# One written sequence for every engine in an mLSTM and gated feed-forward kernel

## The chip, the cores and the metric

The kernel runs on one core of one Trainium2 chip. The metric is the device time of one execution in microseconds (us). TensorE (PE) multiplies matrices into PSUM; VectorE (DVE), ScalarE (ACT) and GpSimd (POOL) do elementwise work; SyncE (SP) issues almost all transfers. Each engine runs its own instructions in the order in which the program has them and waits on semaphores for the others. So what this case is about is only the order.

## The reference

Two stages follow each other. The first is a recurrence over 768 time steps for 4 batches of 8 heads with 40 channels; the second is a gated feed-forward layer over the resulting 3072 tokens of 320 channels.

```python
m_new = np.maximum(f_gate[:, :, t] + m, i_gate[:, :, t])
f_stab = np.exp(f_gate[:, :, t] + m - m_new)
i_stab = np.exp(i_gate[:, :, t] - m_new)
C = f_stab[...] * C + i_stab[...] * np.einsum('bhd,bhe->bhde', vt, kt)
n = f_stab[...] * n + i_stab[...] * kt
h_tilde = np.einsum('bhde,bhe->bhd', C, qt)
denom = np.maximum(np.abs(np.einsum('bhd,bhd->bh', n, qt)[:, :, None]), 1.0)
y[:, :, t] = 1.0 / (1.0 + np.exp(-o_gate[:, :, t])) * h_tilde / denom
...
x = attn_out.transpose(0, 2, 1, 3).reshape(B * S, H * D)
gate = 1.0 / (1.0 + np.exp(-(x @ w_gate)))       # 320 x 1536
return (gate * (x @ w_val) @ w_out).astype(np.float32)
```

The weights arrive as 64-bit floats and are decoded on the chip.

## The kernel before

The 768 steps are cut in 6 chunks of 128, and a chunk c with a batch b is a unit; there are 24, numbered u = 4c + b. In a name such as `ks_0_2055` the 0 is the batch and the last number counts buffers. Within a unit the recurrence is worked as matrix products. `st_a` transposes q and k on TensorE (tile `pt`, in three groups of heads). For chunks 0 and 1 the copies are float32 (`qk`, `qbd`). From chunk 2 on they are split in a high and a low part (`kh` on ScalarE, `kl` on VectorE), and SyncE stores both to a scratch tensor `scr` in DRAM and reads them back stacked (`stack`: `ks`, `qs`). `st_b` forms the scores (tile `s`), which VectorE multiplies with the decay matrix `d`; that one is loaded from `mscr`, exponentiated on ScalarE or prepared on GpSimd, and masked on GpSimd. `st_c` adds the old state's part (`in`) and the gather over the unit's own steps (`av`), divides, and makes `x`. `st_d` transposes `x` (tile `xt`) and splits it into `xh` and `xl`, the feed-forward input. `st_e` updates the state `cst` through tile `cs`.

The feed-forward runs in tiles: `ffn_up` makes two products of 16 matmuls in the PSUM tiles `pg0` and `pg1`, ScalarE takes the tanh of pg0 (`sg`), VectorE multiplies with pg1, ScalarE casts (`gh`), VectorE takes the rest (`gl`), and `ffn_down` adds three matmuls per token block to `po`. A full tile has 512 tokens of a chunk; some chunks are cut in half tiles of 256, first for batches 0 and 1, then for 2 and 3. `pg0` and `pg1` have one buffer each. All other PSUM tiles of the recurrence share the two banks of the pool `ps_a`. The weights come in 30 pieces, each decoded by `w_dec`: a pass on ScalarE (`dc`), three on VectorE, a cast on ScalarE (`wh`, the two halves of `w`, `oh`), a subtraction on GpSimd (`wl`, `w`, `ol`).

What sets the order: TensorE's order is written by hand, as a sort of events by the numbers in `PARAM['pe']` (how far the feed-forward has come). The other engines' order is left to a scheduler with priorities (`PARAM['pri']`), except in the opening (the units 0 and 1 and the first three weight pieces), where `PARAM['open']` ranks the steps, and up to the point `PARAM['pin']`. A step such as `w_dec` or `st_c` was called as one, or from one yield to the next, and the scheduler then placed its instructions.

Of the kernel before, what the change touches and what calls it, by code (L numbers as in the profile page):

```python
# [23 lines left out]
    'pos': {  # L24
# [18 lines left out]
    'pin': 0.9829449281013305,  # L43
    'open': {
# [9 lines left out]
        'wvd': 56.338, 'na1': 103.682, 'xt0': 93.253, 'wve': 83.362, 'wrb': 81.994, 'nb1': 87.717, 'wrc': 83.39,  # L54
        'xt1': 75.16, 'wrd': 105.028, 'wre': 108.438, 'kw1': 88.729, 'e2': 123.641,
    },
    'AV': 4,
    'AV0': 4,
    'up': 0.6550267155341185,
    'pri': {  # L60
        'a': 1, 'b': 62, 'c': 0, 'd': 96, 'u': 1,
    },
    'wllate': [0],
    'split': [0, 0, 0, 5, 5, 5],
# [37 lines left out]
    },  # L102
}
GROUPS = ((0, 3), (3, 3), (6, 2))
# [3 lines left out]
def mlstm_then_gated_ffn_kernel(  # L108
# [36 lines left out]
    ps_a = ctx.enter_context(tc.tile_pool(name="ps_a", bufs=2, space=bass.MemoryType.PSUM))  # L145


# [9 lines left out]
    def load_unit(c, b, eng=nc.sync):  # L157
        t0 = c * L

        def src(t):  # L160
            return t[b, :, t0 : t0 + L, :].rearrange("h t d -> t h d")

        u = (c, b)
        qt[u] = big.tile([P, H, D], F32, tag="q", name=f"q_{c}_{b}", bufs=3)
        kt[u] = big.tile([P, H, D], F32, tag="k", name=f"k_{c}_{b}", bufs=3)
        vt[u] = big.tile([P, H, DA], F32, tag="v", name=f"v_{c}_{b}", bufs=3)
        ot[u] = big.tile([P, H, D], F32, tag="o", name=f"o_{c}_{b}", bufs=3)
        eng.dma_start(qt[u], src(q))
        nc.sync.dma_start(kt[u], src(k))
        eng.dma_start(vt[u][:, :, :D], src(v))  # L170
        nc.sync.dma_start(ot[u], src(o_gate))
        nc.gpsimd.memset(vt[u][:, :, D : D + 1], 1.0)
# [205 lines left out]
    def st_a(c, b):  # L378
# [42 lines left out]
        if not unscored:  # L421
            stack()
# [561 lines left out]
```

## Time and profile before

| | us |
|---|---|
| median of 3 runs (568.5 to 571.63) | 569.81 |
| the profiled execution, its own time | 572.92 |
| its span, first to last instruction | 571.2 |
| TensorE busy | 533.2 (93%) |
| VectorE busy | 320.1 (56%) |
| ScalarE busy | 234.1 (41%) |
| GpSimd busy | 159.7 (28%) |

The mean granted TensorE clock is 0.967 of full speed. A line of the profile names a line of the kernel, the engine, the operation and its tiles (out<-in). Behind an instruction, brackets give how long its engine was idle ahead of it and what ended that. The clock column of the views by stretches is the mean granted clock there: 0.50 is half speed.

### The profile page before, as it was taken

Reading aid. Unit: us, or ns where it says so; the run is one execution under the profiler, and the core shown is the slowest. Engines: PE = TensorE matmul, PEld = TensorE weight load, DVE = VectorE, ACT = ScalarE, POOL = GpSimd, SP = SyncE. Lnnn points to the kernel's source line nnn. Section 1 sums busy time; section 2 is a strip of 40 time slices with the busy share of each in tenths; the row PEclk is TensorE's granted clock in tenths of the full one; section 3 lists DMA queues with packets and bytes.
Section 4 is the critical chain, followed back from the end, with each engine's and each line's share of the span. In section 5 each row is a group of like instructions: output and inputs, shape, how many; then the busy total and the mean of one; then the engine's idle time right before and its main releaser. Section 6 shows DMA issues by size and latency. Waiting matters only on the chain.

```text
span 571.2 us, 12202 instructions
## 1 busy us (share of the span) xinstructions
PE 533.2 (93%) x4739; PEld 477.9 (84%) x4739; DVE 320.1 (56%) x739; ACT 234.1 (41%) x581; POOL 159.7 (28%) x231
## 2 busy tenths in 40 slices
PE   8547899899998989999999999999999999999997
PEld 7346797688797989999888888888888888899996
DVE  5798778874852555463655554554643545533322
ACT  5386556644532335343434242343332332232222
POOL 5567435653712006220142220143210210000000
PEclk9678799999997999999999999999999999999999
DMA  9697647222554556745566765666763734010000
GB/s 198 184 240 221 176 137 207 59 77 53 136 174 88 145 124 165 156 143 123 138 148 154 151 177 134 143 147 143 164 174 107 185 79 110 27 36 2 24 2 23
DMA packets 131649, 72.42 MB, mean 127 GB/s; under 512 B 103112, under 2 KB 120776, under 8 KB 131592
## 3 DMA queue, kind: packets, MB, share of 16 engines
q1 hardware_dynamic: 130504, 71.39, 51.2%
q8 instruction: 37, 0.61, 0.5%
q10 hardware_dynamic: 1088, 0.26, 0.2%
q14 instruction: 20, 0.16, 0.1%
HBM read 56.95 MB, written 14.68 MB: 125 GB/s over the span
## 4 chain that ended last, share of the span: by engine, by line
PE 75%; DVE 8%; DMA 5%; POOL 4%; ACT 3%; issue 3%; SPq 1%; POOLq 0%; DVEq 0%; ACTq 0%
PE pg L585 32%; PE pg L590 11%; PE po L610 7%; PE po L614 6%; PE po L612 6%; DMA qs<-scr 4%; PE s L477 2%; PE av L446 2%; PE pt L408 2%; PE in L491 2%; PE xt L533 2%; PE cs L545 1%; DVE dc L297 1%; DVE dc L302 1%; DVE d L469 1%
## 5 line engine op out<-in xcount | busy, mean ns | idle before, releaser
L585 PE MATMUL pg<-xh,wh 128*128 128x256 f32 (+1 forms) x412 | 111.0, 343 | 4.2 <-ACT sg L594 3.0
L585 PE MATMUL pg<-xh,wl 128*128 128x256 f32 (+1 forms) x412 | 108.9, 340 | 0.0
L595 DVE SCALAR_TENSOR_TENSOR sg<-sg,pg 128x256 f32<-128x256 f32 (+1 forms) x103 | 54.1, 525 | 97.0 <-ACT sg L594 96.3
L585 PE MATMUL pg<-xl,wh 128*128 128x256 f32 (+1 forms) x412 | 106.9, 336 | 0.0
L594 ACT ACTIVATE sg<-pg 128x256 f32<-128x256 f32 (+1 forms) x103 | 48.2, 468 | 128.6 <-PE pg L590 128.1
L610 PE MATMUL po<-oh,gh 128*128 128x320 f32 x288 | 91.8, 319 | 0.8 <-ACT gh L598 0.8
L612 PE MATMUL po<-ol,gh 128*128 128x320 f32 x288 | 91.8, 319 | 0.0
L614 PE MATMUL po<-oh,gl 128*128 128x320 f32 x288 | 91.8, 319 | 0.0
L599 DVE TENSOR_TENSOR gl<-sg,gh 128x256 fp32r<-128x256 f32 (+1 forms) x103 | 60.6, 589 | 38.6 <-ACT gh L598 37.8
L585 PEld LDWEIGHTS pg<-xh,wh 128*128 128x128 f32 x412 | 70.9, 194 | 9.2 <-ACT sg L594 4.0
L585 PEld LDWEIGHTS pg<-xh,wl 128*128 128x128 f32 x412 | 70.5, 193 | 6.4
L585 PEld LDWEIGHTS pg<-xl,wh 128*128 128x128 f32 x412 | 70.4, 193 | 6.3
L598 ACT ACTIVATE gh<-sg 128x256 fp32r<-128x256 f32 (+1 forms) x103 | 51.7, 502 | 50.4 <-DVE sg L595 50.0
L610 PEld LDWEIGHTS po<-oh,gh 128*128 128x128 f32 x288 | 55.2, 192 | 3.2 <-ACT gh L598 1.3
L612 PEld LDWEIGHTS po<-ol,gh 128*128 128x128 f32 x288 | 55.1, 191 | 1.1
L614 PEld LDWEIGHTS po<-oh,gl 128*128 128x128 f32 x288 | 55.4, 192 | 0.6 <-DVE gl L599 0.3
L590 PE MATMUL pg<-xh,w 128*128 128x256 f32 (+1 forms) x206 | 53.8, 339 | 1.5 <-POOL w L341 1.5
L590 PE MATMUL pg<-xl,w 128*128 128x256 f32 (+1 forms) x206 | 52.5, 334 | 0.0
L478 DVE TENSOR_TENSOR d<-s,d 128x384 f32<-128x384 f32 (+1 forms) x48 | 24.1, 510 | 29.1 <-PE s L477 28.6
L262 POOL TENSOR_TENSOR d<-at,d 128x1024 f32<-128x1024 f32 x16 | 30.4, 1899 | 33.3 <-DMA d<-mscr 30.3
L590 PEld LDWEIGHTS pg<-xh,w 128*128 128x128 f32 x206 | 34.4, 193 | 4.3 <-POOL w L341 1.7
L590 PEld LDWEIGHTS pg<-xl,w 128*128 128x128 f32 x206 | 35.0, 192 | 3.2
(126 smaller groups left out, 762.5 us busy)
## 6 DMA issues: line engine op xcount, KB each, us to landing
d<-mscr SPq DMA_DIRECT2D x22, 512.0 KB
ks<-scr SPq DMA_DIRECT2D x16, 360.0 KB
qs<-scr SPq DMA_DIRECT2D x16, 360.0 KB
k<-in_k_dram SPq DMA_DIRECT2D x24, 160.0 KB
v<-in_v_dram SPq DMA_DIRECT2D x24, 160.0 KB
o<-in_o_gate_dram SPq DMA_DIRECT2D x24, 160.0 KB
st_o<-in_moe_w_out_dram SPq DMA_DIRECT2D x12, 320.0 KB
out_dram<-ob SPq DMA_DIRECT2D x24, 160.0 KB
```

The lines of the kernel that those rows point to most:

```text
L262: E(arg).tensor_tensor(d, a, d, ALU.subtract)
L408: nc.tensor.transpose(pt[:r, x, :], t[u][:, h0 : h0 + nh, :].rearrange("p h d -> p (h d)"), ident)
L478: nc.vector.tensor_tensor(dm[u][:, h0 : h0 + nh, :], ps[:, :nh, :], dm[u][:, h0 : h0 + nh, :], ALU.mult)
L585: nc.tensor.matmul(pg[x], w[x][:, a, fs], y[c][:, a, n0:n1], start=x not in began, stop=False)
L590: nc.tensor.matmul(pg[x], w2[x][:, fs], y[c][:, 2, n0:n1], start=False, stop=y is xl)
L594: nc.scalar.activation(sg, pg[0], AF.Tanh, scale=0.5)
L595: nc.vector.scalar_tensor_tensor(sg, sg, 1.0, pg[1], ALU.add, ALU.mult)
L598: last = nc.scalar.activation(gh[u][:, :nt], sg, AF.Copy)
L599: E('gl0' if c == 0 else 'gl').tensor_tensor(gl[u][:, :nt], sg, gh[u][:, :nt].bitcast(F32), ALU.subtract)
L610: nc.tensor.matmul(po[t], g1[:, ts], oh[:, j, :], start=(j == 0), stop=False)
L612: nc.tensor.matmul(po[t], g1[:, ts], ol[:, j, :], start=False, stop=False)
L614: nc.tensor.matmul(po[t], g0[:, ts], oh[:, j, :], start=False, stop=(j == NF - 1))
```

## The change

The order of every engine is written out as one text, `ORDER`, of 3086 words that stand for about 4500 steps; a word with `*n` takes the next n steps of that name. Every function now only puts its small steps in lists by name (`put`), and at the end the words call them one after the other under `tc.manual_schedule()`, now without an engine, so that it holds for all of them. Steps that were one call are split: a weight piece into ScalarE's pass, three on VectorE, the cast, the subtraction and the next load; a unit's gather, its denominators and its product; each store of `kh` and `kl`. The loads of q, k, v and o of a unit are four steps, and so are the reads of `ks` and `qs`. The pool `ps_a` has two tiles by name, `pa0` and `pa1`, taken in turn; the word `/`, 28 times, skips one. The tile `t1` is handled in the same way, without skips. The numbers of matmuls, elementwise instructions and transfers stay the same.

```diff
-    'pe': {
-        'a2': [0.46919, 0.4692, 0.79921], 'a3': [1.06395, 1.10646, 1.10647], 'a4': [2.15465, 2.41214, 2.41215],
...
+ORDER = """
+ib iw ii if lq0 im ie lk0 x0 ig*2 it ia ir ig*2 lk1 w25f lq1 is x1 w26f ic igs iz w21f lo0 gc iac lv0 gc*4 sp00 tr00
...
-    ps_a = ctx.enter_context(tc.tile_pool(name="ps_a", bufs=2, space=bass.MemoryType.PSUM))
+    ps_a = ctx.enter_context(tc.tile_pool(name="ps_a", bufs=1, space=bass.MemoryType.PSUM))
+    last = {"pa": 1, "t1": 1}
+
+    def other(x):
+        last[x] = 1 - last[x]
+
+    def bank_tile(shape, name):
+        other("pa")
+        return ps_a.tile(shape, F32, tag=f"pa{last['pa']}", name=name)
...
+    todo = {}
+
+    def put(key, f, *args):
+        todo.setdefault(key, []).append((f, args))
...
-    with tc.manual_schedule(engines={mybir.EngineType.PE}):
-        with tc.manual_schedule():
-            opening()
...
+    with tc.manual_schedule():
+        for word in ORDER.split():
+            if word == "/":
+                other("pa")
+                continue
+            key, _, n = word.partition("*")
+            for _ in range(int(n or 1)):
+                f, args = todo[key].pop(0)
+                f(*args)
```

Three places show what moves. The first is ScalarE around the tanh of the very first tile (`sg_0_0`); `d_2` and `d_3` are the decay matrices of units 2 and 3, x8 is one exponential for each head. Before:

```order
L259 ACTIVATE d_2_180<-d_2_180,at 128x128 x8
L292 ACTIVATE dc_0_455<-st_o_141 128x320
L292 ACTIVATE dc_1_465<-st_o_432 128x320
L557 ACTIVATE cst<-cs_0_485,rmask 120x2x41 x3
L557 ACTIVATE cst<-cs_0_485,rmask 80x41 x2
L557 ACTIVATE cst<-cs_1_494,rmask 120x2x41 x3
L332 ACTIVATE oh<-dc_0_455 128x320
L332 ACTIVATE oh<-dc_1_465 128x320
L557 ACTIVATE cst<-cs_1_494,rmask 80x41 x2
L292 ACTIVATE dc_1_503<-st_1_139 128x512
L259 ACTIVATE d_3_443<-d_3_443,at 128x128 x8
L594 ACTIVATE sg_0_0_550<-pg_0_0_0_532 128x256
```

After, on the same engine:

```order
L362 ACTIVATE d_2_291<-d_2_291,at 128x128 x4
L450 ACTIVATE oh<-dc_0_452 128x320
L362 ACTIVATE d_2_291<-d_2_291,at 128x128 x4
L407 ACTIVATE dc_1_522<-st_1_412 128x512
L811 ACTIVATE sg_0_0_525<-pg_0_0_0_454 128x256
L445 ACTIVATE wh_98<-dc_1_410 128x2x256
L523 ACTIVATE qk_2_536<-pt_0_2_468 120x256
L450 ACTIVATE oh<-dc_1_471 128x320
L676 ACTIVATE o_2_345<-o_2_345 128x320
L523 ACTIVATE qk_2_536<-pt_0_2_556 80x256
L818 ACTIVATE gh_0_0_562<-sg_0_0_525 128x256
L362 ACTIVATE d_3_481<-d_3_481,at 128x128 x8
```

The exponentials of unit 3 moved from ahead of the first tanh to behind the cast `gh` that follows it, and one of the two casts `oh` also moved behind it.

The second place is SyncE at the units 8 and 9, the first two whose q and k pass through DRAM (`scr_85` is unit 8's scratch, `scr_86` unit 9's). Before:

```order
L419 DMA scr_85<-kl_0_2013 80x1x256
L419 DMA scr_86<-kh_1_2095 80x1x256
L439 DMA ks_0_2055<-scr_85 40x3x384
L437 DMA ks_0_2055<-scr_85 80x3x384
L419 DMA scr_86<-kh_1_2095 40x768 x2
L419 DMA scr_86<-kl_1_2096 40x768 x2
L419 DMA scr_86<-kl_1_2096 80x1x256
L437 DMA qs_0_2056<-scr_85 80x3x384
L439 DMA qs_0_2056<-scr_85 40x3x384
```

After, on the same queue:

```order
L586 DMA ks_0_2076<-scr_85 80x3x384
L586 DMA ks_0_2076<-scr_85 40x3x384
L853 DMA out_dram<-ob_3_2059 128x320
L255 DMA v_1_2106<-in_v_dram 128x8x40
L586 DMA qs_0_2139<-scr_85 80x3x384
L586 DMA qs_0_2139<-scr_85 40x3x384
L255 DMA o_2_2203<-in_o_gate_dram 128x8x40
L255 DMA v_2_2213<-in_v_dram 128x8x40
L557 DMA scr_86<-kh_1_2125 40x768
```

The two reads of `qs` for unit 8 moved ahead of all stores of unit 9. A little later in the same queue an output store stands between the two `qs` reads of unit 9:

```order
L586 DMA ks_1_2382<-scr_86 80x3x384
L586 DMA ks_1_2382<-scr_86 40x3x384
L586 DMA qs_1_2423<-scr_86 80x3x384
L853 DMA out_dram<-ob_2_2426 128x320
L586 DMA qs_1_2423<-scr_86 40x3x384
```

Before, the four reads of unit 9 followed each other.

The third place is TensorE at unit 9's gather (`av_1`). Before, its transpose (`xt_1`) came next:

```order
L614 MATMUL po_1_2088<-oh,gl_11_0_2564 128x320
L585 MATMUL pg_1_1_2_2641<-xh_1400,wh_98 128x256 x2
L446 MATMUL av_1_2645<-v_1_1870,d_1_1877 32x41 x32
L533 MATMUL xt_1_2687<-ident,x_1_2684 128x128 x3
L585 MATMUL pg_1_1_2_2641<-xh_1400,wl_99 128x256 x2
```

After, feed-forward matmuls follow the gather:

```order
L599 MATMUL av_1_2625<-v_1_2106,d_1_1867 32x41 x32
L798 MATMUL pg_1_1_2_2658<-xh_1474,wh_98 128x256 x2
L798 MATMUL pg_1_1_2_2658<-xh_1474,wl_99 128x256 x2
L798 MATMUL pg_1_1_2_2658<-xl_1512,wh_98 128x256 x2
L833 MATMUL po_1_2019<-ol,gh_11_0_2606 128x320
L798 MATMUL pg_1_1_2_2670<-xh_1474,wh_101 128x256 x2
L833 MATMUL po_1_2019<-oh,gl_11_0_2608 128x320
L798 MATMUL pg_1_1_2_2670<-xh_1474,wl_102 128x256
```

The transpose `xt_1` stands eleven rows below the last of these, behind the whole half tile. On GpSimd, the two subtractions of the third weight piece's second column block (`w_100` and `w_103`), which had a product for k and one for `qbd` between them, now follow each other.

More of the change, by code (lines that the diff above doesn't have):

```diff
@@ new lines, in gate_transpose, with turn, take @@
+    def gate_transpose(key, src, dst, c0, c1, func):
+        pt = {}
+        def turn():
+            pt[0] = bank_tile([P, c1 - c0, BH], f"pt_{key}_")
+            for c in range(c0, c1):
+                nc.tensor.transpose(pt[0][:, c - c0, :], src[:, c * L : (c + 1) * L], ident[:BH, :BH])
+        def take():
+            if func is None:
+                nc.vector.tensor_copy(dst[:, c0:c1, :], pt[0])
+            else:
+                nc.scalar.activation(dst[:, c0:c1, :], pt[0], func)
+        put(key, turn)
+        put(key + "c", take)
@@ new lines, in save @@
+        def save(i, m):
+            w = len(range(m, H, 3)) * L
+            p = sop[u][i][m * D : (m + 1) * D].rearrange("p x g t -> p x (g t)")
+            nc.sync.dma_start(scr[b % 2][m, i, :, :, :w], p[:, :, :w].bitcast(F32))
+        for g in range(3):
+            put(f"a{n}.{g}", turn, g)
+            if early:
+                put(f"ah{n}.{g}", copy, g)
+                put(f"aq{n}.{g}", spread, g)
+            else:
+                put(f"ah{n}.{g}", high, g)
+                put(f"al{n}.{g}", low, g)
+                put(f"aq{n}.{g}", keep, g)
@@ new lines, in st_a, with stack, take @@
+        if not early:
+            for i in range(2):
+                for m in range(3):
+                    put(f"as{n}.{3 * i + m}", save, i, m)
+    def stack(c, b):
+        n = c * B + b
+        sc = scr[b % 2]
+        dst = {}
+        def take(x, i, whole):
+            if whole:
+                dst[x] = two.tile([P, 9, L], F32R, tag="b" + "hl"[1 - x], name=f"{'qk'[x]}s_{c}_{b}", bufs=1)
+                rows = slice(i * D, i * D + 2 * D)
+                src = sc[:, :, :, x, :].rearrange("m i d w -> (i d) m w")
+            else:
+                rows = slice((2 - 2 * i) * D, (3 - 2 * i) * D)
+                src = sc[:, 0, :, x, :].rearrange("m d w -> d m w")
+            nc.sync.dma_start(dst[x][rows].rearrange("p (m g) t -> p m (g t)", m=3).bitcast(F32), src)
+            sks[c, b] = dst.get(1), dst.get(0)
+        for x, i in ((1, 0), (0, 1)):
+            put(f"s{n}", take, x, i, True)
+            put(f"s{n}", take, x, i, False)
@@ L471, in st_b @@
[L471 to L480 removed]
+            put(f"bd{n}", d_last, u)
@@ new lines, in st_b, with score @@
+            put(f"bk{n}", k_weight, u)
+        def score(g):
+            h0, nh = GROUPS[g]
+            r = nh * D
+            if c <= PARAM['V32']:
+                qkt, qbd = sop[u]
+                ps[g] = bank(c, b, [P, 3, L], f"s{g}")
+                nc.tensor.matmul(ps[g][:, :nh, :], qkt[:r, g, 1, :], qbd[:r, g, :nh, :], start=True, stop=True)
+            else:
+                ks, qs = sks[u]
+                ps[g] = bank(c, b, [P, 3, L], f"s_{g}")
+                for m in range(nh):
+                    nc.tensor.matmul(ps[g][:, m, :], ks[: 3 * D, 3 * m + g, :], qs[: 3 * D, 3 * m + g, :],
+                                     start=True, stop=True)
@@ L482, in st_c, with times @@
+        def times(g):
+            h0, nh = GROUPS[g]
+            x = dm[u][:, h0 : h0 + nh, :]
+            nc.vector.tensor_tensor(x, ps[g][:, :nh, :], x, ALU.mult)
+        for g in range(3):
+            put(f"b{n}.{g}", score, g)
+            put(f"bm{n}.{g}", times, g)
     def st_c(c, b):
         u = (c, b)
-        nc.scalar.activation(ot[u], ot[u], AF.Tanh, scale=0.5)
-        t1 = None
-        yield
-        if c > 0:
-            pi = bank(c, b, [P, H, DA], "in")
+        n = c * B + b
@@ new lines, in gather, with both @@
+        def gather():
+            t["pv"] = pv = bank(c, b, [P, H, DA], "av")
+            for h in range(H):
+                by_columns(pv[:, h, :], dm[u][:, h, :], vt[u][:, h, :], PARAM['AV'])
+            if c == 0:
+                t["hs"] = pv
+        def both():
+            nc.vector.tensor_tensor(t["hs"], t["hs"], t["pv"], ALU.add)
+        put(f"ct{n}", gate_out, u)
+        if c > 0:
+            put(f"ci{n}", into)
+            put(f"cf{n}", faded)
+            put(f"cs{n}", both)
@@ new lines, in st_d, with turn, high, low @@
+    def st_d(c, b):
+        u = (c, b)
+        n = c * B + b
+        bs = slice(b * L, (b + 1) * L)
+        pt = {}
+        def turn():
+            pt[0] = bank(c, b, [P, 3, L], "xt")
+            for a in range(3):
+                nc.tensor.transpose(pt[0][:, a, :], xin[u][:, a * P : (a + 1) * P], ident)
+        def high():
+            if c not in xh:
+                xh[c] = two.tile([P, 3, NT], F32R, tag="xh", name=f"xh_{c}")
+            nc.scalar.activation(xh[c][:, :, bs], pt[0], AF.Copy)
+        def low():
+            if c not in xl:
+                xl[c] = two.tile([P, 3, NT], F32R, tag="xl", name=f"xl_{c}")
+            nc.vector.tensor_tensor(xl[c][:, :, bs], pt[0], xh[c][:, :, bs].bitcast(F32), ALU.subtract)
+        put(f"d{n}", turn)
+        put(f"dx{n}", high)
+        put(f"dy{n}", low)
@@ L580, in ffn_up, with mm @@
             order = [(x, i) for x in range(2) for i in (0, 1, 2)]
-        began = set()
+        def mm(x, w, y, a):
+            first = x not in pg
+            if first:
+                pg[x] = ps_o.tile([P, NT], F32, tag=f"pg{x}", name=f"pg{x}_{c}_{j}_{t0}")[:, :nt]
+            nc.tensor.matmul(pg[x], w[:, a, fs] if a < 2 else w[:, fs], y[c][:, a, n0:n1],
+                             start=first, stop=a == 2 and y is xl)
         for x, i in order:
-            w, y = terms[i]
+            w, y = ((wh, xh), (wl, xh), (wh, xl))[i]
@@ L584, in ffn_up @@
             for a in range(2):
[L585 to L587 removed]
+                put(f"t{n}", mm, x, w[x], y, a)
         for y in (xh, xl):
             for x in range(2):
[L590 to L593 removed]
@@ L602, in ffn_down, with mm @@
+        for key, f in (("ta", tanh), ("tg", gate), ("th", high), ("tl", low)):
+            put(f"{key}{n}", f)
     def ffn_down(n):
         c, j, t0, t1 = tiles[n]
-        if j == 0:
-            for t in range(t0, t1):
+        def mm(t, g, o, first, last):
+            if j == 0 and first:
                 po[t] = ps_o.tile([P, DM], F32, tag=f"po{t}", name=f"po{t}_{c}")
-        g1, g0 = gh.pop((c, j, t0)), gl.pop((c, j, t0))
+            nc.tensor.matmul(po[t], g[c, j, t0][:, (t - t0) * P : (t - t0 + 1) * P], o[:, j, :],
+                             start=j == 0 and first, stop=j == NF - 1 and last)
@@ L679, in opening, with resets @@
-        pw = ps_o.tile([P, NT], F32, tag="pg1", name="pwarm")
-        for n in range(PARAM["warm"]):
-            nc.tensor.matmul(pw[:, :P], warm[:, :P], warm[:, :P], start=True, stop=True)
+                put("iz", nc.sync.dma_start, sc[2, i, :, :, 2 * L :],
+                    warm[D : 2 * D].rearrange("p (x t) -> p x t", x=2))
+        def resets():
+            nc.gpsimd.memset(mend[:, 0:1], -1e30)
+            nc.gpsimd.memset(m0, 0.0)
+            nc.gpsimd.memset(rst, 1.0)
+            nc.gpsimd.memset(rst.rearrange("p (c l) -> p c l", l=L)[:, :, 0:1], 0.0)
@@ new lines, in small_masks, with warming @@
+        def small_masks():
+            nc.gpsimd.tensor_copy(rmask, bmask[:, :, 0])
+            nc.gpsimd.memset(sel, 1.0)
+            nc.gpsimd.affine_select(out=sel, in_=sel, pattern=[[0, P]], compare_op=ALU.is_ge,
+                                    fill=0.0, base=-(L - 1), channel_multiplier=1)
+        put("ir", resets)
+        put("it", make_identity, nc, ident)
+        put("ib", block_mask, bmask, L)
+        put("ic", block_mask, cmask, DA)
+        put("is", small_masks)
+        def warming():
+            pw = ps_o.tile([P, NT], F32, tag="pg1", name="pwarm")
+            for n in range(PARAM["warm"]):
+                nc.tensor.matmul(pw[:, :P], warm[:, :P], warm[:, :P], start=True, stop=True)
@@ new lines, in mlstm_then_gated_ffn_kernel @@
+    for n in range(len(tiles)):
+        ffn_up(n)
+        ffn_down(n)
+    for u in range(NU):
+        c, b = divmod(u, B)
+        for n in range(4):
+            put(f"l{'qkvo'[n]}{u}", load, (c, b), n, nc.scalar if u == n == 0 else nc.sync)
+        put(f"v{u}", last_column, (c, b))
+        if u > 1:
+            put(f"ld{u}", dmat_load, c, b)
+            st_a(c, b)
+            if c > PARAM['V32']:
+                stack(c, b)
+            st_b(c, b)
+            st_c(c, b)
+            st_d(c, b)
+            dmat(f"e{u}", c, b)
+        if c < NCH - 1:
+            st_e(c, b)
+        store(c, b)
```

824 lines of the change are left out of this document (381 added, 443 removed), and 50 rows, old and new, of the table PARAM.

## The prediction

> **What bounds the kernel now.** I read the page first, then the busy times by stretches, then TensorE's waits in the worst stretches, then the timelines there and the chain of waits.
>
> ```profile
> span 571.2 us, 12202 instructions
> PE 533.2 (93%) x4739; PEld 477.9 (84%) x4739; DVE 320.1 (56%) x739; ACT 234.1 (41%) x581; POOL 159.7 (28%) x231
> ```
>
> TensorE is busy 93%, so at most 38 us are idle. The next view cuts the span in stretches. After the stretch and its length it gives PE, PEld, DVE, ACT and POOL busy (instructions), then the granted clock, the DMA share and GB/s.
>
> ```profile
> 0.00:28.00 28.00, 19.17 (x209) 15.81 (x209) 18.35 (x44) 12.45 (x34) 15.18 (x37) 0.84 0.85 188
> 28.00:70.00 42.00, 29.66 (x267) 24.97 (x268) 37.47 (x77) 28.86 (x88) 26.00 (x32) 0.78 0.80 209
> 70.00:120.00 50.00, 47.25 (x319) 39.43 (x318) 40.64 (x88) 30.45 (x77) 27.12 (x30) 0.96 0.48 132
> 120.00:173.00 53.00, 51.87 (x515) 46.15 (x514) 32.24 (x77) 24.66 (x66) 21.70 (x28) 1.00 0.45 119
> 173.00:210.00 37.00, 31.48 (x342) 30.41 (x341) 17.39 (x46) 10.88 (x29) 5.12 (x12) 0.91 0.53 115
> 210.00:570.00 360.00, 353.74 (x3095) 321.16 (x3093) 173.96 (x411) 126.75 (x291) 64.57 (x93) 1.00 0.48 114
> ```
>
> TensorE's idle time (length less busy) is 8.8, 12.3, 2.8, 1.1, 5.5 and 6.3 us. From 210 on it is the bound and little can be had. The opening (0 to 70) and 173 to 210 hold 27 of the 37 us, and there the clock is below 1.00 as well. But from 28 to 70 VectorE is busy 37.47 of 42, so that stretch can shrink by no more than 4.5 us while VectorE's work keeps its durations. What TensorE waits for there, in total, times and longest:
>
> ```profile
> PE pg L585 <- ACT sg L594: 2.8, 1, 2.8
> PE ptg L228 <- ACT cst L557: 2.2, 1, 2.2
> PE pt L391 <- DVE at L230: 2.0, 1, 2.0
> PE pg L590 <- POOL w L341: 1.5, 1, 1.5
> ```
>
> **The change, step by step.** The same 3803 matmuls, 739 VectorE instructions and 348 SyncE transfers are issued by both kernels; nothing is removed or added. So every term is a wait that goes, stays or comes. The sum is made against the profiled execution (572.92 us, span 571.2) and then put on the median, 569.81, which lies 3.1 lower.
>
> *Opening up to the first gated tile, 0 to 28.* The order of the two first units is nearly kept. VectorE's long stall also keeps its causes: four tensor products in a row on GpSimd stand beside a 0.41 us tensor_scalar that took 3.62.
>
> ```profile
> 6.94 0.41 DVE L297 TENSOR_SCALAR dc<-dc 128x512 f32<-128x512 f32 x1
> 14.63 3.62 DVE L297 TENSOR_SCALAR dc<-dc 128x512 f32<-128x512 f32 x1
> ```
>
> In the new order the second tensor_scalar of that weight piece (0.4 us alone) still stands ahead of unit 1's products and beside the same four GpSimd instructions. The bounds are +0.4 (ScalarE has a weight decode ahead of the first exponentials now, a pass like the 0.41 above) and -3.2 (the stall gone); I take -1, nearer to the kept stall.
>
> *Tile 0 to tile 1.* Tile 1's first matmul needs tile 0's tanh, since pg0 is one buffer. These are ScalarE's rows and VectorE's rows between unit 1's transpose and that tanh:
>
> ```profile
> 26.93 0.49 ACT L535 ACTIVATE xh<-xt 128x384 fp32r<-128x384 f32 x1 [3.43 <-PE xt L533]
> 37.46 2.45 ACT L259 ACTIVATE d<-d,at 128x128 f32<-128x128 f32 x8 [0.24 <-DMA d<-mscr]
> 39.82 0.36 ACT L594 ACTIVATE sg<-pg 128x256 f32<-128x256 f32 x1
> 40.23 0.58 PE L585 MATMUL pg<-xh,wh 128*128 128x256 f32 x1 [2.83 <-ACT sg L594]
> 27.45 0.56 DVE L536 TENSOR_TENSOR xl<-xt,xh 128x384 fp32r<-128x384 f32 x1 [1.29 <-ACT xh L535]
> 36.00 1.40 DVE L222 TENSOR_TENSOR gin<-mend,mg 32x512 f32<-32x512 f32 x1
> 37.44 0.42 DVE L393 COPY qk<-pt 120x256 f32<-120x256 f32 x1
> 40.21 0.42 DVE L595 SCALAR_TENSOR_TENSOR sg<-sg,pg 128x256 f32<-128x256 f32 x1
> ```
>
> The eight exponentials of unit 3 (2.45 us) go behind tile 0's cast, so the tanh may come 2.45 us earlier. VectorE's multiply may come 1.40 + 0.42 = 1.8 us earlier, since these two now stand behind it. The earliest transposes of unit 2 get the other PSUM bank than the gate transpose and move ahead of it, inside tile 0. That ends the 2.2 and 2.0 us waits, but they lay ahead of the same tanh and are not counted twice. Bounds: -1.8 (VectorE) and -2.45 (ScalarE); I take -2.3, since the tanh comes last. What is late next is tile 2, which wants the low half of the third weight piece from GpSimd:
>
> ```profile
> 50.12 0.74 POOL L341 TENSOR_TENSOR w<-dc,w 64x256 fp32r<-64x256 f32 x1
> 50.94 0.85 POOL L455 TENSOR_TENSOR k<-k,dl 128x320 f32<-128x320 f32 x1
> 51.75 1.19 POOL L396 TENSOR_TENSOR qbd<-qk,bmask 120x384 f32<-120x384 f32 x1
> 53.01 0.94 POOL L341 TENSOR_TENSOR w<-dc,w 64x256 fp32r<-64x256 f32 x1
> ```
>
> The new order has its two halves back to back, without the 0.85 and 1.19 between them; that covers the 1.5 us wait. Bounds 0 and -1.5; I take -1.2. Together 28 to 70 gains 3.5, inside VectorE's 4.5.
>
> *70 to 120.* VectorE is busy 40.64 of 50, TensorE idles 2.8. The first of unit 4's three scores moves 4 us of gated matmuls ahead of the other two, which it had stood beside. Bounds 0 and -2.8; I take -1, because VectorE is nearly full.
>
> *The score of unit 8, 173 to 183.* SyncE's rows, the landing from the chain of waits, TensorE's wait, the stretch after it with its clock, and two like matmuls that begin two half tiles in a row:
>
> ```profile
> 167.88 0.67 SPq L419 DMA_DIRECT2D scr<-kh  x2
> 168.60 1.56 SPq L419 DMA_DIRECT2D scr<-kl  x3
> 170.20 0.50 SPq L437 DMA_DIRECT2D qs<-scr  x1
> 170.75 5.37 DMA qs<-scr
> 176.37 1.51 PE L477 MATMUL s<-qs,ks 120*128 120x128 f32 x6 [2.74 <-DMA qs<-scr]
> 176.40:183.00 6.60, 6.60 (x29) 6.60 (x30) 2.46 (x5) 1.27 (x3) 0.87 (x2) 0.50 0.31 54
> 169.23 0.41 PE L585 MATMUL pg<-xh,wh 128*128 128x256 f32 x2
> 172.03 0.41 PE L585 MATMUL pg<-xh,wh 128*128 128x256 f32 x2
> ```
>
> Unit 8's two reads of qs stood behind unit 9's five stores, which ran from 167.88 to 170.16. Now they stand ahead of all of unit 9's stores, with one output store and one load between them and the ks reads. The reads are issued some 2.3 us earlier (170.20 less 167.88), and the score's place is 0.9 us of matmuls later, by the order. That is 3.2 us against a wait of 2.74, so it goes: -2.7. With it goes the half clock: 6.60 us at 0.50 hold 3.3 us of work, another -3.3. Bounds: 0 (the reads wait for an output store) and -6.0; I take -6.0.
>
> [...]
>
> *The transpose of unit 9, near 207.*
>
> ```profile
> 204.73 0.82 PE L446 MATMUL av<-v,d 128*32 128x41 f32 x64
> 207.76 0.61 PE L533 MATMUL xt<-ident,x 128*128 128x128 f32 x3 [2.21 <-DVE x L522]
> ```
>
> The transpose followed its gather at once and waited 2.21. Now a half tile stands between them (2.80 us from 169.23 to 172.03). Bounds 0 and -2.2; I take -2.0, since one tile's low half now stands in VectorE's chain.
>
> *210 to 570.*
>
> ```profile
> PE pg L585 <- ACT xh L535: 1.2, 2, 0.6
> PE s L477 <- DMA qs<-scr: 0.9, 2, 0.7
> ```
>
> At two chunk boundaries the last transpose moves about 1 us of matmuls earlier, which covers the 1.2. For the last unit of the later chunks, 1 to 4 us more of matmuls stand between its last transpose and its first score, which covers the 0.9. Bounds 0 and -2.1; I take -2.
>
> *New waits.* Some 4500 steps are placed anew and I followed a few. The nearest row is 210 to 570: 6.3 us idle in 360, which is 10 over the whole span. Bounds: 10, and -3 for waits relieved unseen in the opening; I take 4.
>
> Sum: -1 -3.5 -1 -6 -2 -2 +4 = -11.5. Profiled 572.9 becomes 561.4, and the median 569.8 becomes 558.3.
>
> **The rivals.**
>
> *More than that.* In 28 to 70 the mean clock 0.78 means 18.5 us at half speed (0.22 x 42 / 0.5). TensorE is busy 29.66 of 42 there, so 6.5 us go to the slow clock. If the shorter waits keep the clock up, 6 to 8 more are gained: about 551. Against it: VectorE's 37.47 of 42.
>
> *VectorE takes the opening back.* Its order changes little from 28 to 120, so the 4.5 us there may not come, and new waits may be 8 instead of 4: 567, hardly a change. For it: its busy share of 89% there.
>
> *Slower: one SyncE queue, whose reads wait behind a store.* In the new order the second qs read of unit 9 stands behind the output store of token block 2, which waits for VectorE. Such stores wait long:
>
> ```profile
> SPq L622 <- DVE ob L618: 80.2, 6, 32.1
> ```
>
> The mean is 13.4 us. Should one such wait fall on that read, unit 9's score and all behind it on TensorE wait as long, and the clock costs 3.3 as above: +16.7, or 575. It decides from a wait of 8.2 us on, since 8.2 + 3.3 eat the 11.5. Against it: that store's halving now stands early on VectorE, ahead of unit 9's products.
>
> [...]
>
> **How the numbers follow.** About 0.5% (2.8 us) is what a measurement of this kernel can tell from no change. [...] More (545 to 555): 0.22. VectorE takes it back (562 to 571): 0.21. Slower by a queue or by several lesser waits (above 571): 0.15. Below 567 lie the first two and half of the third, less a little: 0.73; within 0.5%: 0.12; above 572.7: 0.15. The range leaves out the best of the second case and the fourth: 548 to 571.
>
> **What would show it.** Right: no wait of TensorE above 1 us between tile 0 and tile 1 other than for the tanh, whose start is 2 us or more earlier; the unit 8 score without a wait for qs and the clock at 1.00 behind it; unit 9's transpose within 0.5 us; 210 to 570 idle below 5 us. Wrong: waits of TensorE for ks, qs or x above 2 us at other units, the granted clock below 1.00 past 120 us, or VectorE busy over 90% up to 120 with the same idle time of TensorE.

## The result, and the profile after

| | before | after |
|---|---|---|
| median, lowest, highest (us) | 570.7, 568.5, 572.4 | 541.8, 541.7, 542.3 |
| span of the profiled execution (us) | 571.2 | 540.0 |
| mean granted clock | 0.967 | 0.990 |

The ratio is 0.950, with a 95% interval of 0.946 to 0.953: 29 us less, where 11.5 were forecast. The time lies below the range. The head of the page of after, and then the same stretches as in the prediction (stretch, length, PE, PEld, DVE, ACT and POOL busy, clock, DMA share, GB/s):

```profile
span 540.0 us, 12183 instructions
...
PE 519.3 (96%) x4739; PEld 469.3 (87%) x4739; DVE 317.7 (59%) x739; ACT 230.2 (43%) x581; POOL 163.3 (30%) x231
```

```profile
0.00:28.00 28.00, 22.93 (x234) 19.04 (x234) 20.05 (x52) 15.52 (x47) 18.29 (x38) 0.94 0.94 213
28.00:70.00 42.00, 32.16 (x319) 27.15 (x319) 35.80 (x81) 30.37 (x89) 29.52 (x35) 0.92 0.87 213
70.00:120.00 50.00, 49.95 (x393) 42.43 (x392) 43.02 (x89) 33.85 (x86) 29.84 (x32) 1.00 0.53 142
120.00:173.00 53.00, 52.98 (x570) 50.17 (x569) 33.87 (x87) 22.22 (x62) 18.25 (x27) 1.00 0.58 138
173.00:210.00 37.00, 37.00 (x416) 36.63 (x416) 22.04 (x60) 15.75 (x42) 15.44 (x23) 1.00 0.74 169
210.00:539.90 329.90, 324.33 (x2820) 293.87 (x2818) 162.91 (x374) 112.51 (x258) 51.92 (x77) 1.00 0.48 112
```

TensorE's idle time is now 5.1, 9.8, 0.1, 0.0, 0.0 and 5.6 us, 20.6 in all, where it was 36.8. Of the 31.2 us of span, 16 are idle time. Another 11 are matmuls that no longer run at half clock: 29.2 us of TensorE's busy time lay in half-clock stretches before and 7.0 lie there now, and half of each is taken as loss (14.6 and 3.5), an estimate from the granted 0.50: in before the 128x256 matmuls of L585 start 0.21 us apart at half clock (181.94 to 182.80 us) and 0.12 at full (172.03 to 172.99 us), which would make it some 10 instead of 11. Another 1 is idle time behind 570 us of before, at the kernel's end. The other 3 are not assigned. The profiled execution of before has a low clock among its own (0.967, where 19 executions on one chip had 0.967 to 0.981), so the clock's share is probably smaller in most of its executions.

Since work has moved between the stretches, the gain is better read at equal progress of the gated feed-forward. The first column counts nominal microseconds of its matmuls that TensorE has begun (each with its length at full clock, about 0.12 us for 256 columns and 0.15 for 320); the others are worked out from the start times in the two traces.

| feed-forward begun | before | after | gain so far | what lies ahead of it |
|---|---|---|---|---|
| 0.1 | 29.2 | 24.2 | 5.0 | the opening |
| 5.2 | 48.0 | 43.3 | 4.7 | tiles 0 to 2 |
| 11 | 70.9 | 60.6 | 10.3 | units 2 and 3 |
| 44 | 118.2 | 102.4 | 15.8 | units 4 and 5 |
| 66 | 149.2 | 134.1 | 15.1 | |
| 84 | 179.4 | 157.5 | 22.0 | unit 8's score |
| 102 | 209.0 | 181.7 | 27.3 | unit 9's transpose |
| 395 | 565.8 | 535.4 | 30.5 | the rest |

What TensorE still waits for from 24 to 56 us, the larger part of what is left of its waits (total, times, longest):

```profile
PE pg L798 <- ACT sg L811: 4.7, 3, 3.4
PE pt L508 <- DVE d L635: 1.5, 1, 1.5
PE pt L508 <- DVE at L321: 1.2, 1, 1.2
PE s L624 <- DVE d L635: 1.1, 1, 1.1
```

Ahead of the first gated matmul, two long waits of before (3.4 and 2.4 us) have become one of 2.2. Before, then after, from 0 to 120 us:

```profile
PE xt L533 <- POOL x L522: 4.2, 2, 3.4
...
PE av L446 <- DVE d L748: 2.7, 2, 2.4
```

```profile
PE xt L719 <- POOL x L697: 2.2, 1, 2.2
```

### The profile page after: what moved, and what is told of

Its sections match the earlier page's. It is cut to its first block, busy times and chain, and to the rows that moved or that the text cites. A ratio compares the mean times of both kernels' runs of the same rounds, so it can differ in the third digit from the quotient of the medians.

```text
span 540.0 us, 12183 instructions
## 1 busy us (share of the span) xinstructions
PE 519.3 (96%) x4739; PEld 469.3 (87%) x4739; DVE 317.7 (59%) x739; ACT 230.2 (43%) x581; POOL 163.3 (30%) x231
## 4 chain that ended last, share of the span: by engine, by line
PE 84%; DMA 6%; DVE 4%; SPq 3%; ACT 1%; issue 1%; POOL 0%; DVEq 0%; POOLq 0%; ACTq 0%
PE pg L798 48%; PE po L833 22%; PE av L599 3%; DMA qs<-scr 3%; PE pt L508 3%; PE s L629 2%; PE in L650 2%; PE cs L751 2%; PE s L624 1%; PE xt L719 1%; DMA st_o<-in_moe_w_out_dram 1%; DVE gl L822 1%; SPq L255 1%; DMA q<-in_q_dram 1%; DMA scr<-warm 1%
## 5 line engine op out<-in xcount | busy, mean ns | idle before, releaser
L798 PE MATMUL pg<-xh,wh 128*128 128x256 f32 (+1 forms) x412 | 112.3, 339 | 5.0 <-ACT sg L811 4.7
L798 PE MATMUL pg<-xh,wl 128*128 128x256 f32 (+1 forms) x412 | 110.9, 336 | 0.0
L798 PE MATMUL pg<-xl,wh 128*128 128x256 f32 (+1 forms) x412 | 109.3, 335 | 0.0
L833 PE MATMUL po<-ol,gh 128*128 128x320 f32 x288 | 90.6, 317 | 0.0
L822 DVE TENSOR_TENSOR gl<-sg,gh 128x256 fp32r<-128x256 f32 (+1 forms) x103 | 64.7, 628 | 27.6 <-ACT gh L818 27.4
L798 PEld LDWEIGHTS pg<-xh,wl 128*128 128x128 f32 x412 | 69.8, 191 | 4.4
L798 PE MATMUL pg<-xl,w 128*128 128x256 f32 (+1 forms) x206 | 58.5, 329 | 0.0
L833 PEld LDWEIGHTS po<-oh,gl 128*128 128x128 f32 x288 | 54.0, 188 | 3.9 <-DVE gl L822 0.9
L702 POOL COPY x<-x 128x64 f32<-128x64 f32 x22 | 6.2, 280 | 153.8 <-DVE x L697 132.0
L635 DVE TENSOR_TENSOR d<-s,d 128x384 f32<-128x384 f32 (+1 forms) x66 | 32.9, 508 | 29.6 <-PE s L629 29.0
L367 POOL TENSOR_TENSOR d<-at,d 128x1024 f32<-128x1024 f32 x16 | 30.6, 1914 | 28.1 <-DMA d<-mscr 28.0
L798 PEld LDWEIGHTS pg<-xl,w 128*128 128x128 f32 x206 | 36.2, 189 | 2.2
```

The costliest lines, as they stand in the source:

```text
L367: E(arg).tensor_tensor(d, a, d, ALU.subtract)
L635: nc.vector.tensor_tensor(x, ps[g][:, :nh, :], x, ALU.mult)
L798: nc.tensor.matmul(pg[x], w[:, a, fs] if a < 2 else w[:, fs], y[c][:, a, n0:n1], start=first, stop=a == 2 and y is xl)
L822: E('gl0' if c == 0 else 'gl').tensor_tensor(gl[u][:, :nt], sg[0], gh[u][:, :nt].bitcast(F32), ALU.subtract)
L833: nc.tensor.matmul(po[t], g[c, j, t0][:, (t - t0) * P : (t - t0 + 1) * P], o[:, j, :], start=j == 0 and first, stop=j == NF - 1 and last)
```

## The experiments

The sequence is text, so the order of before can be written in it too, and any part of either order. That is what most of the runs do: moving words, no instruction more or less. Times are medians; before has 570.2 to 571.8 beside them. After was timed once (four executions) and not again beside each run, so a difference of under 1 us from its 541.8 tells nothing.

**The order alone, and the opening.** seq_before is the new program with the words sorted so that each engine's order is that of before (a few neighbours on ScalarE, GpSimd and SyncE apart, since a step is not split). opening_before takes the words up to the first gated matmul from it and the rest from after; opening_after is the converse.

> The new form of the program (one list of steps, banks named) with the order of every engine as it was before the change. If the order is what made the 29 us, this takes what the kernel before takes, 568 to 574 us. If the form itself (which buffer a tile gets, which semaphores an instruction waits for) has a part in it, it comes out under 565 us, and by that much the order has less to explain.

> Everything up to the first gated matmul in the order of before, everything from there on in the order of after. In the traces the first gated matmul starts 5.0 us earlier after the change (24.2 for 29.2 us). If the opening's gain is its own and is kept, this takes 5 us more than the changed kernel, 546 to 548 us. If waits later on would have taken the gain back or hidden the loss (the rival that the prediction named: VectorE is the bound up to 70 us), it stays within 1.5 us of 541.8.

> The other half: the opening in the order of after, the rest as before. If the gains of the stretches add up, 570.7 - 5 = 565 to 567 us. If VectorE holds the stretch up to 70 us, where it was busy for 37.5 of 42 us before the change, the 5 us are given back there and this takes 569 us or more.

Measured: seq_before 574.6, ratio to before 1.004 (1.002 to 1.007); opening_before 547.3; opening_after 573.1, ratio 1.000 (0.997 to 1.003). The form itself gives nothing, it costs some 2.5 to 4 us (574.6 here, 575.5 for 571.3 on another chip); the text `ORDER` gives all. Beside the order that text holds the 28 skipped banks of after, of which seq_before has none; what they give by themselves was not tried. The new opening is worth 5.6 us ahead of the new rest, and 1.5 ahead of the old one. In opening_before the first gated matmul starts at 27.0 us, only 2.8 later than in after; the rest of the 5.6 is lost behind it, most of it by 55 us. In opening_after the first gated matmul starts at 24.1 us, 5.3 earlier than in seq_before, but tile 1 then waits for a tanh on ScalarE; opening_after, 24 to 44 us:

```profile
PE pg L797 <- ACT sg L810: 6.8, 1, 6.8
PE pt L507 <- DVE mend L1028: 2.7, 1, 2.7
```

**Three single undos in the changed kernel, and one step of the opening.**

```diff
 decode_back:  - lk2 lq2 wvb qb10 ti02 iz      + lk2 lq2 qb10 ti02 wvb iz
 exp_back:     - w6b ta0 ... e3*2 tl0          + w6b e3*2 ta0 ... tl0
 unit8_back:   - s8*2 t19 ta19 ... as9.4       + t19 ta19 ... as9.4 s8*2
 unit9_back:   - c9 t29*2 ... cx9 ... d9       + c9 ... cx9 d9 t29*2 ...
```

> The changed kernel with one step moved on VectorE alone: the first tensor_scalar of the second weight piece (dc, 128x512, 0.44 us at 14.26 us) goes behind the product of unit 1's second score, to where GpSimd's products stand back to back (14.85 to 18.80 us). Theory: the opening's 5 us are this step, which took 3.62 us beside four GpSimd products before the change and made unit 1's last products 2.4 us late; it is held up again for 3 us or more and the kernel takes 544.5 to 547. Rival: the opening gains by the whole of its order, and this step alone costs under 1 us (at most 542.8).

> The changed kernel with unit 3's eight decay exponentials (2.44 us on ScalarE) put back ahead of the first tanh. Theory: tile 1 waits for that tanh, so TensorE loses 2.4 us, and up to 5 where the exponentials themselves wait for their DMA (4.41 us in opening_after): 544 to 547. Rival: VectorE is what holds the stretch up to 70 us, and the later tanh is absorbed there: under 1 us.

> The changed kernel with unit 8's two qs reads put back behind unit 9's six stores on SyncE, as before the change. Theory: the score waits for them again, 2 to 4 us, and where the wait fills more than half of one stretch of the clock's grid (3.41 us, by the times at which the granted clock changed in six runs) another 1.7 to 3.4 us are lost to half clock: 544 to 548. Rival: matmuls of the tiles fill the wait, since the reads are issued four matmul groups ahead: under 1 us.

> The changed kernel with unit 9's transpose put right behind its gather on TensorE again (the half tile between them goes behind it). Theory: TensorE waits for the normalisation, 2.4 us as before the change, plus up to 1.7 us where the wait fills most of a stretch of the clock's grid: 544 to 546. The rival that the prediction left room for: the wait of before was a late VectorE and not the place of the transpose, and then it is under 1 us.

Measured: 542.0, 546.0, 549.6 and 544.9, so 0.2, 4.2, 7.8 and 3.1 us. exp_back and unit9_back come out as their theories say. unit8_back has the mechanism of its theory, but costs more than the 548 that it gave as the most: the wait is 5.6 us, where 2 to 4 were expected, and two stretches of the clock behind it run at half speed (the means of 0.80 and 0.71 over 7 us each make 6.9 us at 0.50). Their waits of TensorE, one kernel after the other, and the clock behind unit 8's wait:

```profile
PE pg L795 <- ACT sg L808: 8.5, 2, 8.1
```

```profile
PE s L626 <- DMA qs<-scr: 5.6, 1, 5.6
```

```profile
156.00:163.00 7.00, 1.37 (x8) 1.14 (x7) 0.42 (x1) 0.80 (x2) 0.00 (x0) 0.80 0.56 151
163.00:170.00 7.00, 7.00 (x43) 7.00 (x43) 2.71 (x6) 1.18 (x3) 0.00 (x0) 0.71 0.01 2
```

```profile
PE xt L716 <- DVE x L694: 2.6, 1, 2.6
```

The waits of 8.1 and 5.6 are longer than those of before (2.83 and 2.74): an undo in the new order isn't the old order, since all that stands around it has moved too.

decode_back did not bring its cost back, and the trace shows why. The step and the GpSimd product beside it, start and length, in after (with the next pass of the same weight piece, L416), in decode_back and in opening_before:

```profile
14.26 0.44 DVE L412 TENSOR_SCALAR dc<-dc 128x512 f32<-128x512 f32 x1
...
14.85 1.18 POOL L947 TENSOR_TENSOR qbd<-qk,bmask 120x384 f32<-120x384 f32 x1
...
15.42 0.89 DVE L416 TENSOR_SCALAR dc<-dc 128x512 int32<-128x512 int32 x1
```

```profile
14.57 1.00 POOL L944 TENSOR_TENSOR qbd<-qk,bmask 120x384 f32<-120x384 f32 x1
...
14.80 1.05 DVE L409 TENSOR_SCALAR dc<-dc 128x512 f32<-128x512 f32 x1
```

```profile
13.63 2.40 DVE L409 TENSOR_SCALAR dc<-dc 128x512 f32<-128x512 f32 x1
...
15.03 0.72 POOL L605 TENSOR_TENSOR k<-k,dl 128x320 f32<-128x320 f32 x1
```

In decode_back it ends at 15.85, 0.28 behind the first product (15.57), and in opening_before at 16.03, 0.28 behind the third (15.75). In after it begins ahead of the products and takes 0.44, and the next pass is held instead, for 0.89, until 0.28 behind the first product (16.03). So decode_back held the two passes for some 1.0 us in all, against 0.5 in after and 3.2 in before. It shows that the step's place costs little here; what a hold of 3 us costs it does not test.

**GpSimd's row of products broken in the old order.** The wl product (wge) goes behind unit 0's x:

```diff
- ti12 ct0 wge sc11 ti10 ti11 c1 cv0*3 cg0 cr0 cx0
+ ti12 ct0 sc11 ti10 ti11 c1 cv0*3 cg0 cr0 wge cx0
```

> seq_before with one GpSimd product (wl of the first piece, 1.26 us) moved behind the product that makes unit 0's x. VectorE's 128x512 tensor_scalar ended 0.28 to 0.30 us behind the last of GpSimd's products that stood back to back, in four runs (18.25, 18.44, 16.03, 16.89 us). Theory: it now ends at about 16.9, unit 1's products come 1.3 to 2.4 us earlier, and the first gated matmul starts 1.3 to 2.4 us earlier. At the end of the kernel between nothing and all of it is left, since tile 1 waits for a tanh that does not depend on it: 572 to 574.6. Rival: the 3.62 us have another cause (its operand comes late), and the time of that instruction does not change.

Measured: 575.0. The step takes 2.32 instead of 3.62 us and ends at 17.58, 0.28 behind the product that is now the last of the row:

```profile
15.26 2.32 DVE L411 TENSOR_SCALAR dc<-dc 128x512 f32<-128x512 f32 x1
...
16.58 0.72 POOL L607 TENSOR_TENSOR k<-k,dl 128x320 f32<-128x320 f32 x1
```

That fits the theory on the hold, but is no proof of it: in before_unit8_filled (below), which leaves wl in the row, VectorE was let in behind the same third product, after 2.41 us, and its next pass was held for wl instead (1.37 us). The rival, a late operand, does not fit an end 0.28 to 0.30 us behind a product each time. The forecast of an earlier start was wrong: the first gated matmul began at 29.6 us (29.4 in seq_before). The moved product held up the next step that it met, the copy of x, for 1.24 us instead of 0.20. Part of the hold went to another place. No run takes it away altogether, so what it costs by itself stays open; what was measured is the opening's order as a whole.

**The middle.** middle_back has the order of before from the third half tile to the seventeenth tile step (44 to 103 us of after), middle_first only to the sixth half tile; the words around are those of after.

> The changed kernel with every engine's order of before from the third half tile (about 44 us) to the seventeenth tile step (about 103 us), and that of after ahead of it and behind it. The four single moves and the opening account for 20.6 us (5.5 + 4.2 + 7.8 + 3.1) of the 29; in the traces another 8.4 us lie here (TensorE's waits 3.5 us fewer, half clock 5.0 us less). Theory: they come back as a whole, 549 to 552. Rival: they were a consequence of the late first tanh, and with that early the order of this stretch costs under 3 us (at most 544.8).

> As middle_back (553.4), but in the order of before from the third half tile to the sixth only (44 to about 66 us). In its trace 5.7 of the 11.6 us were lost by the seventh half tile and the rest between 75 and 115 us. If the two halves have causes of their own (transposes of units 2 and 3 and the half clock they bring; products of units 4 and 5), this takes 547 to 548.5. If the second half follows from the first (pieces and units that come late), it takes 551 or more.

Measured: 553.4 and 547.9, so 11.6 and 6.2 us: two causes of about the same size. From 44 us on, the same progress (up to 44 us of it) took 69.8 us in middle_back and 58.4 in after, in two parts each, cut at 16 us of progress:

```profile
44.00:73.00 29.00, 23.80 (x253) 21.14 (x254) 21.49 (x51) 15.87 (x46) 16.46 (x21) 0.82 0.77 203
73.00:113.80 40.80, 38.05 (x265) 30.44 (x264) 35.35 (x75) 27.42 (x69) 23.55 (x26) 1.00 0.46 122
```

```profile
44.00:66.40 22.40, 19.00 (x249) 16.70 (x250) 19.13 (x50) 15.49 (x44) 14.44 (x19) 1.00 0.86 218
66.40:102.40 36.00, 35.95 (x264) 30.50 (x263) 33.13 (x71) 25.43 (x64) 22.48 (x25) 1.00 0.57 152
```

The first part is 6.6 us longer: 5.2 us idle against 3.4, and the rest is busy time, at a clock of 0.82 against 1.00. The second is 4.8 longer at full clock: 2.8 idle against 0.1, and 2.1 more of busy time, which is not assigned. The waits of middle_back from 40 to 120 us name the places, the transposes of units 2 and 3 and the decays of the state behind them, then the products of units 4 and 5:

```profile
PE s L622 <- DVE d L633: 1.8, 3, 0.9
PE xt L717 <- DVE x L695: 1.8, 1, 1.8
PE pt_cdec L335 <- DVE xl L727: 1.6, 1, 1.6
PE xt L717 <- POOL x L700: 1.3, 1, 1.3
```

Which single move ends which of these was not tried.

**The clock.** before_unit8_filled puts ten matmuls into unit 8's wait in seq_before; filled puts 26 into three waits of after, at 20.5, 28.0 and 29.6 us, the two longest among them.

```diff
+                if n == 8 and g == 0:
+                    for m in range(10):
+                        nc.tensor.matmul(ps[g][:, 0, :], ident, ident, start=True, stop=True)
```

> seq_before with ten matmuls of the identity with itself, about 2.5 us at full clock, put in front of unit 8's first score product, so that TensorE works while it waits for the 2.74 us at 173.6 us. The wait stays. If the half clock of the 6.9 us behind it comes from the idle time, it goes, and the kernel takes 3.3 us less than seq_before, about 567. If the clock falls for another reason (the power of all engines, or the time since the last fall), nothing changes, or it costs up to 1 us.

> The changed kernel with matmuls of the identity with itself (8, 5 and 13 of 0.24 us at full clock) in TensorE's three longest waits, 20.5, 28.0 and 29.6 us. The waits stay; nothing else is moved. Theory of the clock: a stretch of the 3.41 us grid that is less than half busy sets the next to half clock; with the waits filled none of the three half stretches (23.8 to 27.2, 30.6 to 37.5 us) is left, the work in them that nothing else holds up (2 to 4 us behind 33.3) goes twice as fast, and the kernel takes 1.5 to 2.5 us less: 539.3 to 540.3. Rival: the clock does not follow the matmul queue's idle time, or the fillers themselves make the next work late: 541.5 to 543.

Measured: 575.8 and 542.4. The first won nothing. In seq_before's profiled execution there was nothing to win, since the same wait cost no clock. But the mean granted clock over ten executions is 0.972 in both as well, so this run does not show that filling a wait keeps the clock up. Stretches of 3.4 us around it, in before and in seq_before:

```profile
172.70:176.10 3.40, 0.93 (x8) 0.73 (x7) 0.28 (x1) 0.77 (x1) 2.49 (x5) 1.00 1.13 180
176.10:179.50 3.40, 3.13 (x14) 3.17 (x15) 1.54 (x3) 0.85 (x2) 0.30 (x1) 0.51 0.58 102
```

```profile
173.10:176.50 3.40, 2.27 (x18) 2.07 (x16) 0.85 (x2) 1.62 (x3) 1.15 (x2) 1.00 1.02 212
176.50:179.90 3.40, 1.99 (x16) 2.02 (x16) 1.02 (x2) 0.70 (x2) 1.63 (x4) 1.00 1.07 153
```

In before the wait fell into one stretch, which left it 27% busy, and the next was at half clock. In seq_before it was cut in two, 67% and 59% busy, and the clock stayed. The profiled execution of seq_before loses one stretch at unit 9's transpose instead (TensorE busy for 1.19 of 3.40 us from 203.9 to 207.3 us, then a clock of 0.50 up to 210.7), where that of before loses none (1.00 from 183 to 210 us). filled does show the clock following TensorE: of the three half-clock stretches of after (23.8 to 27.2 and 30.6 to 37.5 us) one is left (40.1 to 43.5), and at 3.6 us of progress it is 1.8 us ahead of after. But at 7 us of progress both are at 50 us, so something else holds the start.

**A version that beats both?**

```diff
 tanh0_early:  - e2 g h0c ... w6b ta0 ... tg0    + ta0 e2 g h0c tg0 ... w6b ...
 early_filled: the same; ta1 ahead of e3*2, tg1 behind tl0, fillers of 8 and 5 matmuls
```

> The changed kernel with the first tanh moved further ahead on ScalarE, in front of unit 2's eight decay exponentials, and its gate product behind the copy at 29.2 us on VectorE. The second tile waits 3.59 us for that tanh. Theory: what is left of the start is ScalarE's order, and 2 to 3.5 us go: 538.3 to 540. Rival: VectorE (35.8 of 42 us busy between 28 and 70) decodes the pieces that the next tiles need no earlier, and at most 1 us goes: 540.8 or more.

> The two together: first tanh early, the second tanh ahead of unit 3's exponentials too, fillers (8 and 5) at 20.5 and 28.0 us. If both theories hold, 536 to 539. If VectorE is the bound of the start, as in the rival of tanh0_early, the tiles wait for weight pieces instead and it is 539.5 to 541.5.

Measured: 541.3 and 542.9; neither differs from the changed kernel's 541.8 by what can be told. tanh0_early has 2 us of progress at 29.1 instead of 33.6 us and has given it back by 44. From 24 to 56 us it now waits for the copies of a unit's q and k; filled, shown behind it, for VectorE's low half of a tile:

```profile
PE pt L505 <- ACT qk L520: 3.6, 2, 3.2
...
PE po L830 <- DVE gl L819: 1.4, 1, 1.4
```

```profile
PE po L830 <- DVE gl L819: 2.0, 1, 2.0
PE pg L795 <- ACT sg L808: 1.7, 2, 1.1
```

Three kernels, each relieved in another way, reach 7 us of progress between 49.6 and 51.4. So what holds the start up to there is not one wait of TensorE. That it is VectorE (35.80 of 42 us busy) fits, and was not shown by a run.

**The three moves that the prediction priced, in both orders.** three_moves makes them in seq_before, but there GpSimd copies unit 3's last column ahead of its exponentials, so it computes something else, and nothing is concluded from its time; three_moves_2 makes them too, with unit 3's last column taken behind its exponentials; three_back undoes all three in the changed kernel. seq_again is seq_before on that chip.

> seq_before (the old order in the new form, 574.6) with only the three moves that the prediction priced: unit 3's decay exponentials behind the first gh cast, unit 8's qs reads ahead of unit 9's stores, unit 9's transpose half a tile behind its gather. By the single undo runs (4.2 + 7.8 + 3.1) 559.5 if they add up; by the prediction's own terms (2.3 + 6.0 + 2.0) 564. Rival: in the old order other waits stand behind them, as with the opening, where 5.3 us at the first tile left 1.5 at the end: 567 or more.

> seq_before once more, beside the next run on the same chip: 572 to 576. It is the value that three_moves_2 is taken from.

> three_moves with unit 3's last column taken behind its exponentials (in three_moves GpSimd copied that column ahead of them, so that unit 3's contribution to the state was computed from other values). Three_moves took 571.9, 2.7 us less than seq_before, where the single undo runs add up to 15.1. If that holds, the moves are worth 2 to 5 us in the old order and the rest of their worth hangs on what stands around them; if the wrong copy had cost time, 559 to 566.

> The same three undone together in the changed kernel: exponentials, unit 8's reads, unit 9's transpose. Each alone cost 4.2, 7.8 and 3.1 us. Nothing that one of them makes late is used by the next before TensorE has caught up, so they should add up: 556 to 558. Rival: a late start leaves the later waits covered, as in the old order: 553 or less.

Measured: 571.9; then 575.5, 572.5 and 559.1. In the new order they add up to a little more than singly, 17.3 us for 15.1. In the old order they are worth 2.9 (575.5 less 572.5). There the tanh's 3.5 us are gone by 5.2 us of progress, and unit 8's reads uncover a wait for a tanh just behind the score. TensorE's waits from 170 to 215 us, of seq_again (unit 8's score, unit 9's transpose) and then of three_moves_2. For the score the view names the load of v, which SyncE issued right behind the reads of qs; the matmul itself reads qs and ks:

```profile
PE s L628 <- DMA v<-in_v_dram: 2.2, 1, 2.2
PE xt L718 <- DVE x L696: 2.2, 1, 2.2
```

```profile
PE pg L797 <- ACT sg L810: 1.5, 1, 1.5
```

## Why the prediction was wrong

The forecast was 555 to 562 us, at a chance of 0.42. In its sum, single waits of TensorE give 12.2 us, new waits take 4, and the half clock behind unit 8's score gives 3.3. In the two profiled executions TensorE's idle time fell by 17 us and the loss to half clock by 11. The steps that failed lie for the most part up to 120 us: the sum took the gain there as a few single waits, put the half clock there at nothing (7.8 of the 11 us came from there), and allowed 4 us for new waits, of which little came. By term:

- *Opening*, -1: measured -5.0 at the first gated matmul, and -5.6 at the end by opening_before. The step that failed is the stall that was to be nearly kept, since the step "still stands ahead of unit 1's products and beside the same four GpSimd instructions". By the order it does stand there. But the pass that was held in before (3.62 us) now runs 0.6 us ahead of the products, the pass behind it is held for only 0.45 us, and TensorE's two waits of 3.4 and 2.4 us became one of 2.2. The order of two engines does not tell what runs beside what. Which part of the opening's order brings the 5 us stays open: decode_back cost 0.2, and gpsimd_gap started the tiles no earlier.
- *Tile 0 to tile 1*, -2.3: right in kind, since tile 1 starts 7.0 us earlier (33.26 for 40.23), of which 5.0 are the opening and 2.0 the moved exponentials. By 48 us the 2.0 are gone again.
- *28 to 70 and 70 to 120*, -1.2 and -1: measured -5.6 and -5.5 between 5.2 and 44 us of progress, and 11.6 by middle_back. This is the term that was missed by most. Two half-clock falls of before (56.7 to 60.1 and 66.9 to 73.7 us) held 9.9 us of matmuls, so 5 us of loss by the same halving, and the sum put a price on none of it. VectorE's busy time, which held the prediction back here ("VectorE is nearly full"), was no bound either: a busy time is no amount of work. VectorE was busy for 94.7 us up to 44 us of progress before and for 85.9 after, with 201 and 197 instructions.
- *Unit 8*, -6.0: -6.9 between 66 and 84 us of progress, but 3 of these come by 70 us, ahead of the wait. From 82 to 85, with the wait and its half clock, it is -6.3. *Unit 9*, -2.0: -2.9 between 99 and 102. Both mechanisms are right, and each comes back when it is undone (7.8 and 3.1). That unit 8's size fits is partly luck: its 3.3 us of clock were lost in the profiled execution of before, and not in that of seq_before, which has the same order.
- *210 to 570*, -2: -3.2 from 102 us of progress on. Of the two waits named, the one for xh (1.2) is gone and that for qs is 0.5 instead of 0.9; TensorE's idle time up to 395 us of progress fell by 1.3 (3.7 to 2.4), so the rest is not theirs.
- *New waits*, +4: waits of 1.5, 1.0 and 1.1 us stand at 43 to 54 us and lie inside the gain of that stretch; past 63 us only one reaches 1 us (1.0, at 288). So this term is 4 too high.
- The rival "More than that" names what came, the clock from 28 to 70 (0.78 to 0.92), and would have given 551. The opening and the stretch from 70 to 120 came on top. Of the four signs that would show it right, unit 8's and unit 9's held. Two were missed by little: a wait of 1.2 us for VectorE's copy of at stands between tile 0 and tile 1, and 210 to 570 is idle for 5.6 us and not below 5. Of the signs that would show it wrong, one came by its words: TensorE waits 2.2 us for unit 1's x, where it had waited 3.4.

## What to carry to other kernels

Undoing one move in a new order, and making it in the old one, are two different measurements: three moves were worth 17 us in one direction and 3 in the other, because in the traces a move paid only where the next wait had gone too. Read gains at equal progress of the main work, and exchange whole stretches between the two orders: opening, middle and the three moves (5.6 + 11.6 + 17.3) come to 34.5 us, against 33 between seq_before and after. And a wait of 1.5 to 3 us can be worth more than it looks, depending on where the clock's grid of 3.41 us falls: unit 8's wait left TensorE busy for 27% of one stretch in before, and the next 6.8 us were at 0.50; in seq_before, cut in two (67% and 59%), it cost no clock.

## What the hardware showed

- In the traces of before and after the granted clock changes only on a grid: in before at 19.14, 29.38, 36.20, 46.44, 56.68, 60.10, 66.92, 73.75, 176.15 and 182.98 us, in after at 23.81, 27.22, 30.64, 37.46 and 539.22 us, within each trace whole multiples of 3.413 us apart. Its place against the kernel's start differs: counted back, the first edge is at 2.07 us in before and at 3.33 in after. The two traces hold 305 whole stretches of the grid at full clock, from where the records of the clock begin (8.90 and 10.16 us). Eight of them were followed by half clock; TensorE was busy in these for 0.49 to 1.65 us (up to 0.48 of the stretch) and in the other 297 for 2.08 us (0.61) or more. In seq_before a stretch that was 0.59 busy (176.5 to 179.9 us) was not followed by one either. A fall lasted one to three stretches; the last of after runs up to the kernel's end.
- The spread of the times fits this, though no run shows that the grid makes it: before ran from 567.8 to 574.1 us over 19 runs on one chip, and the two with the lowest granted clock (0.967) took 572.4 and 574.1; after ran from 541.7 to 542.3 over 4.
- A pass of VectorE's 128x512 tensor_scalar took 0.44 us by itself (after, 14.26 us). Beside GpSimd's products in the opening it took longer and ended 0.28 to 0.30 us behind the end of one of them, in seven runs: behind the fourth in before and seq_before (3.62 us in each), behind the third in before_unit8_filled (2.41), opening_before (2.40) and gpsimd_gap (2.32), behind the first in decode_back (1.05) and, with the next pass, in after (0.89). In before_unit8_filled it was let in behind the third although the fourth followed without a gap (at 16.59 us). Why it is held, and what decides behind which product it is let in, no run shows.
